# Moving an attention kernel's transposes from TensorE to DMA and its LayerNorm apply from ScalarE to GpSimd

## The chip, the cores and the metric

The kernel runs on one core of a Trainium2 chip. The metric is device time in microseconds (us) of one execution, median over several. Every run quoted here was fast: none was over 1.5% above the fastest run of its kernel.

Words used below: PE is TensorE's matmul, PEld its weight load, DVE is VectorE, ACT is ScalarE, POOL is GpSimd and SP is SyncE. "SPq" and "ACTq" in a profile line are those engines' sequencers issuing a DMA.

## The reference, cut to what matters

Four layers, A B A B, on x of 2048 rows by 576 columns, with x in bf16 and the sums kept in f32:

```python
def _A_ref(x, wqkv, wo):          # attention: 32 heads of 18; a query sees itself and 7 earlier keys, 2 apart
    ...
    idx = pos[:, None] - off[None, :]            # off = 0, 2, ..., 14
    logits = jnp.einsum('bhsd,bhswd->bhsw', q, kg) * scale
    attn = _softmax(jnp.where(mask, logits, -1e9), axis=-1)
    o = jnp.einsum('bhsw,bhswd->bhsd', attn, vg)
    return o.reshape(B, S, D) @ wo

def _B_ref(x, w_in, w_sp, b_sp, w_out):          # mixer
    z = _gelu(x @ w_in)                          # 576 -> 4608
    z1, z2 = z[..., :Fh], _layernorm(z[..., Fh:])
    g = jnp.einsum('ts,bsf->btf', w_sp, z2) + b_sp[None, :, None]
    return (z1 * g) @ w_out

x = x + _A_ref(_layernorm(x), ...)               # then B, then A, then B in the same way
```

## The kernel before

An attention works on tiles of queries against a window of 128 keys. Each tile is done in two steps, one per half of the heads. A step is: scores on PE, Exp on ACT, a multiply with a 0/1 mask on DVE, the product with V on PE, and a normalisation on DVE into `o_t`. The first steps also carry the QKV product and a DMA scatter of Q and K (called "early steps" here). The other 22 steps have Exp split into two halves and "junk" matmuls that keep PE busy ("late steps").

Two transposes happen per tile. The attention output `o_t` is transposed before the output product, and the normalised row `xn` is transposed into `xnT`, the input of the next layer. Before the change both are matmuls against an identity, followed by a DVE copy out of PSUM:

```python
def ln_xn(self, pool, x_t, nrows, rstd, nmr, eng="act"):
    xn = self.bridge.tile([P, 640], bf16, name="ln_xn", tag="ln_xn", bufs=4)
    nc.gpsimd.memset(xn[:nrows, D:640], 0.0)
    if eng == "act":
        nc.scalar.activation(out=xn[:nrows, 0:D], in_=x_t[:nrows, :], func=ACT.Identity,
                             scale=rstd[:nrows, 0:1], bias=nmr[:nrows, 0:1])
    elif eng == "pool":
        nc.gpsimd.tensor_scalar(out=xn[:nrows, 0:D], in0=x_t[:nrows, :], scalar1=rstd[:nrows, 0:1],
                                scalar2=nmr[:nrows, 0:1], op0=ALU.mult, op1=ALU.add)
    ...
def ln_T(self, xn, row0, nrows, evac="dve"):
    tp = self.PT_tile([P, 5, P], bf16, "ln_tp")
    for c in range(5):
        nc.tensor.transpose(tp[:, c, :nrows], xn[:nrows, c * P:(c + 1) * P], self.ident[:nrows, :nrows])
    self.copy_bf16(self.xnT[:, :, PADL + row0:PADL + row0 + nrows], tp[:, :, :nrows], eng=evac)
```

The tail of a tile is spread over the steps after it. TAIL_A transposes `o_t` and loads the residual, TAIL_B makes the output product and the statistics, TAIL_B2 applies the LayerNorm on ACT, and TAIL_C transposes `xn`:

```python
for (off, fn) in ((2, TAIL_A(t)), (3, TAIL_B(t)), (4, TAIL_B2(t)), (6, TAIL_C(t))):
    s_ = plast + off            # steps after the tile's last step
    ...
```

A mixer begins with its input product (lines with `pz`). The first three of its five weight blocks (`win2a`) are loaded long before. The last two (`win2b`) get their space only when the attention's pools close, and one of them is issued on SP and one on ACT:

```python
for c in range(NPF, 5):
    self.dma(win2b[:kc, c - NPF, :], self.B_w_in[...], eng=(nc.sync, nc.scalar)[c % 2])
```

The very first LayerNorm, of the input, is spread over engines too: two row groups of 128 in three are applied on ACT, the third on GpSimd.

The softmax here doesn't subtract the row's maximum and nothing guards it: scores larger than these inputs give would overflow.

## Time and profile before

| | before |
|---|---|
| median of 4 runs | 1367.35 us (1366.06 to 1368.14) |
| profiled execution, span | 1364.2 us |
| PE, DVE, ACT, POOL busy | 92%, 48%, 30%, 20% |

By stage, read from the starts and ends of Exp and of the mixers' matmuls in the timeline (us):

| stage | before |
|---|---|
| start, to the first Exp | 47.6 |
| first attention: early steps / late steps | 66.4 / 72.0 |
| from the end of the last Exp to the end of PE's last wait for `win2b` ("entry") | 17.0 |
| first mixer: input product / spatial product | 78.4 / 330.7 |
| output product and the second attention's QKV | 110.1 |
| second attention: early / late / entry | 63.8 / 71.9 / 15.0 |
| second mixer: input product / rest | 78.4 / 412.9 |

The table of stretches gives for each stretch its length, the busy time and count of PE, PEld, DVE, ACT and POOL, then the clock that was granted to PE, the DMA share and GB/s. These are the start, the late steps and the entry of the first mixer, before:

```profile
0.00:48.00 48.00, 26.67 (x156) 16.84 (x157) 21.69 (x80) 18.57 (x27) 30.50 (x108) 1.00 0.60 183
...
114.00:186.00 72.00, 60.55 (x1052) 47.78 (x1060) 66.08 (x164) 49.78 (x65) 13.17 (x40) 1.00 0.25 66
186.00:203.00 17.00, 8.85 (x66) 6.31 (x67) 9.25 (x24) 3.88 (x4) 2.75 (x8) 0.88 0.41 109
```

In the late steps DVE is busy 66.08 of 72 us and PE 60.55: no engine is quite full. One tile of them in the timeline (columns: start, duration, engine, line and operation, output<-inputs, count, and in brackets how long the engine was idle before it and for whom):

```profile
133.86 1.75 ACT L507 ACTIVATE P_sb_115<-L_ps 128x912 bf16<-128x912 f32 x2 [1.36 <-PE O_ps L540]
...
134.33 0.41 PE L187 MATMUL ln_tp<-ident,ln_xn 114*128 114x114 bf16 x5
...
134.59 0.41 PE L565 MATMUL o_tp<-ident,o_t 114*128 114x114 bf16 x5
...
135.56 0.44 DVE L82 COPY xnT<-ln_tp 128x285 int32<-128x285 int32 x1
...
135.93 0.44 DVE L82 COPY oT_t<-o_tp 128x285 int32<-128x285 int32 x1
...
136.33 0.87 ACT L173 ACTIVATE ln_xn<-x_new,ln_nmr,ln_rstd 114x576 bf16<-114x576 f32 x1 [0.71 <-POOL ln_nmr L164]
...
140.48 0.93 ACT L507 ACTIVATE P_sb_115<-L_ps 128x912 bf16<-128x912 f32 x1 [1.36 <-PE O_ps L540]
```

The same Exp returns after 140.48 − 133.86 = 6.62 us: that is the time of one tile (here and below, the mean over six tiles in the middle of the late steps). Exp waits for PE, PE carries ten transposes, DVE carries two copies of 0.44 us, and ACT itself carries the LayerNorm apply of 0.87 us.

The entry to the first mixer, in the timeline before:

```profile
189.07 2.63 PE L581 MATMUL pw<-wo_sb,oT_t 128*114 128x288 bf16 x10
...
197.75 0.55 SPq L77 DMA_DIRECT2D win2b<-in_B_w_in_dram  x1
197.76 0.35 ACTq L77 DMA_DIRECT2D win2b<-in_B_w_in_dram  x1
...
201.97 0.38 PE L811 MATMUL pz<-win2b,xnT 128*128 128x512 bf16 x1 [3.50 <-DMA win2b<-in_B_w_in_dram]
```

The last weights are issued at 197.75, and PE stands 3.50 us for them, then another 0.67.

Before, the start's GpSimd applies (multiply by `rstd`, add `nmr`) are listed by duration (min/median/max in ns):

```profile
L176 POOL TENSOR_SCALAR ln_xn<-x_in_207,ln_rstd,ln_nmr x2: 820/820/821, 29.7 to 33.3; 128x576 bf16<-128x576 bf16 x2
```

### The profile page before, as it was taken

The numbers are of one execution on the slowest core, as the hardware profiler recorded it, in microseconds if no ns is written. First come the engines' busy times: TensorE is split into PE (matmuls) and PEld (weight loads), VectorE is DVE, ScalarE is ACT, GpSimd is POOL, SyncE is SP. The second block draws the span as 40 slices with busy tenths as digits, with TensorE's granted clock in tenths as the row PEclk, the third lists the DMA queues.
The fourth block names the chain that finished last, engine by engine and source line by source line (L and its number), as shares of the span: only waits on it lengthen the run. The fifth ranks groups of instructions, "written<-read, shape, count | busy, mean of one in ns | idle before, by whom it ended". The sixth has DMA issues, their size and how long they took to land.

```text
span 1364.2 us, 22004 instructions
## 1 busy us (share of the span) xinstructions
PE 1261.8 (92%) x8906; PEld 705.5 (52%) x9008; DVE 653.8 (48%) x1496; ACT 410.5 (30%) x609; POOL 274.5 (20%) x569
## 2 busy tenths in 40 slices
PE   3998869989999999998999888799999999999897
PEld 2566644444444444446865666444444444444476
DVE  5468967853223223333544799688333232332221
ACT  3566647630111111001125666466111111001000
POOL 6422116840000000002241221288100000000011
PEclk9999999999999999997999999999999999999999
DMA  6323239020000000007432332580100000000242
GB/s 211 71 72 85 63 96 230 1 86 9 9 9 10 9 9 9 1 5 247 132 107 69 93 88 80 146 166 18 64 10 9 9 9 5 5 9 0 66 118 65
DMA packets 114469, 85.32 MB, mean 63 GB/s; under 512 B 72616, under 2 KB 96552, under 8 KB 114368
## 3 DMA queue, kind: packets, MB, share of 16 engines
q1 hardware_dynamic: 104548, 68.41, 18.7%
q10 hardware_dynamic: 6364, 8.55, 2.1%
q0 software_dynamic: 3456, 6.96, 2.0%
q8 instruction: 70, 1.15, 0.4%
q14 instruction: 31, 0.25, 0.1%
HBM read 41.16 MB, written 16.52 MB: 42 GB/s over the span
## 4 chain that ended last, share of the span: by engine, by line
PE 66%; DVE 16%; DMA 5%; ACT 5%; POOL 4%; issue 3%; SPq 0%; ACTq 0%; POOLq 0%; DVEq 0%
PE pg L903 35%; PE po L940 9%; PE pp L414 5%; DVE z_junkD L818 4%; DMA QK<-stg 2%; DVE ln_st L157 2%; PE pw L581 1%; POOL z_rstd L834 1%; DMA wout_b<-in_B_w_out_dram 1%; POOL ln_rstd L162 1%; ACT P_sb_116 L507 1%; ACT P_sb_7442 L507 1%; DVE P_sb_7442 L527 1%; DVE x_new L583 1%; PE pv L372 1%
## 5 line engine op out<-in xcount | busy, mean ns | idle before, releaser
L907 DVE TENSOR_TENSOR g_tmp<-pg,bsp 128x512 f32<-128x512 f32 x144 | 99.4, 692 | 434.7 <-PE pg L903 399.1
L811 PEld LDWEIGHTS <-xnT 128*128 128x128 bf16 x800 | 78.1, 98 | 91.9 <-issue 13.7
L414 PE MATMUL pp<-xnT,wqk_sb 128*126 128x512 bf16 (+1 forms) x400 | 100.1, 392 | 6.1 <-ACT xnT L84 4.7
L811 PE MATMUL pz<-win2a,xnT 128*128 128x512 bf16 x380 | 102.6, 379 | 2.0 <-DVE x_new L583 1.6
L811 PE MATMUL pz<-win2b,xnT 128*128 128x512 bf16 x242 | 73.6, 385 | 8.2 <-DMA win2b<-in_B_w_in_dram 7.3
L815 ACT ACTIVATE zp<-pz 128x1024 bf16<-128x1024 f32 x64 | 65.1, 1021 | 51.7 <-POOL z2b_10393 L844 21.9
L414 PEld LDWEIGHTS <-wqk_sb 128*126 128x126 bf16 (+1 forms) x400 | 50.3, 133 | 35.8 <-issue 8.9
L581 PE MATMUL pw<-wo_sb,oT_t 128*114 128x288 bf16 (+1 forms) x360 | 57.4, 297 | 2.1 <-DVE oT_t L82 1.1
L372 PE MATMUL pv<-wv_sb,xnT 128*128 128x288 bf16 x360 | 56.0, 285 | 2.7 <-PE L_ps L492 2.5
L162 POOL TENSOR_TENSOR ln_rstd<-ln_rstd,neg_half 114x1 f32<-114x1 f32 (+1 forms) x68 | 39.2, 578 | 89.1 <-DVE ln_rstd L161 89.0
L818 DVE CUSTOM_DVE_ANT_0 z_junkD<-zp 128x1536 bf16<-128x1536 bf16 x32 | 56.6, 1768 | 1.1 <-ACT zp L815 1.1
L492 PE MATMUL L_ps<-QK 18*128 18x114 bf16 x1152 | 31.9, 212 | 20.0 <-ACT P_sb_7442 L507 5.1
L581 PEld LDWEIGHTS <-oT_t 128*114 128x114 bf16 (+1 forms) x360 | 44.1, 135 | 5.9 <-DVE oT_t L82 1.5
L187 PE MATMUL ln_tp<-ident,ln_xn 114*128 114x114 bf16 (+2 forms) x340 | 29.1, 224 | 17.4 <-ACT ln_xn L173 11.5
L173 ACT ACTIVATE ln_xn<-x_new,ln_nmr,ln_rstd 114x576 bf16<-114x576 f32 (+1 forms) x36 | 31.2, 867 | 46.3 <-POOL ln_nmr L164 46.3
L171 POOL MEMSET ln_xn<- 114x64 bf16 (+1 forms) x68 | 10.8, 161 | 164.2 <-PE ln_tp L187 71.3
L77 POOL DMA_DIRECT2D QK<-stg x52 | 31.5, 606 | 59.8 <-ACT stg L423 43.4
L492 PEld LDWEIGHTS <-QK 18*128 18x128 bf16 x1152 | 21.0, 93 | 43.2 <-issue 38.7
L77 POOL DMA_DIRECT2D wout_b<-in_B_w_out_dram x14 | 7.6, 548 | 172.5 <-PE pg L903 172.5
L372 PEld LDWEIGHTS <-xnT 128*128 128x128 bf16 x360 | 32.6, 97 | 12.6 <-issue 0.4
L82 DVE COPY xnT<-ln_tp 128x285 int32<-128x285 int32 (+2 forms) x60 | 27.3, 458 | 23.6 <-PE ln_tp L187 9.9
L187 PEld LDWEIGHTS <-ln_xn 114*128 114x128 bf16 (+2 forms) x340 | 23.8, 101 | 21.2 <-ACT ln_xn L173 13.4
(504 smaller groups left out, 2558.7 us busy)
## 6 DMA issues: line engine op xcount, KB each, us to landing
xres_74<-x_new SPq DMA_DIRECT2D x17, 256.5 KB
xo<-xres_75 SPq DMA_DIRECT2D x17, 256.5 KB
xres_76<-x_new SPq DMA_DIRECT2D x17, 256.5 KB
QK<-stg POOLq DMA_DIRECT2D x52, 72.0 KB, 3.7
win2a<-in_B_w_in_dram SPq DMA_DIRECT2D x2, 1728.0 KB
QK<-stg SPq DMA_DIRECT2D x48, 72.0 KB
wqk_sb<-in_A_wqkv_dram ACTq DMA_DIRECT2D x4, 576.0 KB
out_dram<-ob SPq DMA_DIRECT2D x16, 144.0 KB
```

Of the source, the lines that this page charges most:

```text
L162: nc.gpsimd.tensor_tensor(out=rstd[:nrows, :], in0=rstd[:nrows, :], in1=self.neg_half[:nrows, :], op=ALU.pow)
L187: nc.tensor.transpose(tp[:, c, :nrows], xn[:nrows, c * P:(c + 1) * P], self.ident[:nrows, :nrows])
L372: nc.tensor.matmul(pv[:, 0:288], lhsT=self.xnT[:, c, QT * t:QT * t + P], rhs=wv_sb[:, c, hh * 288:(hh + 1) * 288], start=(c == 0), stop=(c ...
L414: nc.tensor.matmul(pp[:M, :], lhsT=wqk_sb[:, c, wc0:wc0 + M], rhs=self.xnT[:, c, col0:col0 + 512], start=(c == 0), stop=(c == 4))
L492: nc.tensor.matmul(L_ps[:, j, ftl * QT:(ftl + 1) * QT], lhsT=kT[32 * j:32 * j + DH, g, QT * t:QT * t + P], rhs=qT[32 * j:32 * j + DH, g, Q ...
L581: nc.tensor.matmul(pw[:nq, 0:288], lhsT=oT_t[:, c, :nq], rhs=wo_sb[:, c, hh * 288:(hh + 1) * 288], start=(c == 0), stop=(c == 4))
L811: nc.tensor.matmul(pzvs[ci][:, sub * 512:sub * 512 + w], lhsT=self.xnT[:, c, PADL + i * P:PADL + (i + 1) * P], rhs=win2(c)[:, c0 + sub * 5 ...
L815: nc.scalar.activation(out=zp[:, c0:c0 + cn], in_=pzvs[ci][:, 0:cn], func=ACT.Gelu_apprx_tanh, accum_out=sums[:, ci:ci + 1])
L818: nc.vector.tensor_tensor_reduce(out=junkD[:], in0=zp[:, 0:SQ_D], in1=zp[:, 0:SQ_D], scale=1.0, scalar=0.0, op0=ALU.mult, op1=ALU.add, acc ...
L903: nc.tensor.matmul(pg[:, :], lhsT=z2b[jj][:, i, sub * P:(sub + 1) * P], rhs=W_sb[:, i, q * 512:(q + 1) * 512], start=(i == 0), stop=(i == ...
L907: nc.vector.tensor_tensor(out=tmp[:], in0=pg[:, :], in1=bsp[:, q * 512:(q + 1) * 512], op=ALU.add)
L940: nc.tensor.matmul(acc[hh], lhsT=uT[j // 2][:, j % 2, i * P:(i + 1) * P], rhs=wout_j(j)[:, hh * 288:(hh + 1) * 288], start=(j == 0), stop= ...
```

## The change

The intent is to free PE and DVE of transposes and copies, and ACT of the apply, in the steps where the three are in each other's way. The core of the diff, with cuts:

```diff
-HALO = (W_ATT - 1) * DIL          # 14, so 114 queries per tile
+HALO = 16                         # 112 queries per tile: 19 tiles instead of 18, the last of 32
@@ ln_xn
-        elif eng == "pool":
-            nc.gpsimd.tensor_scalar(out=xn[...], in0=x_t, scalar1=rstd, scalar2=nmr, op0=ALU.mult, op1=ALU.add)
+            e = nc.gpsimd if eng == "pool" else nc.vector
+            e.tensor_scalar(out=xn[...], in0=x_t, scalar1=mv[:nrows, 0:1], scalar2=rstd, op0=ALU.subtract, op1=ALU.mult)
@@ ln_T
-        ... five nc.tensor.transpose and a copy ...
+        self.nc.sync.dma_start_transpose(out=self.xnT[:, :, PADL + row0:PADL + row0 + nrows], in_=xn[:nrows, :])
@@ TAIL_A
-        ... five nc.tensor.transpose and a DVE copy ...
+        nc.sync.dma_start_transpose(out=oT_t[:, :, :nq], in_=o_t[:nq, :])
@@ TAIL_B2
-        st["xn"] = self.ln_xn(sb, x_new, st["nq"], rstd, nmr, eng="act")
+        st["xn"] = self.ln_xn(x_new, st["nq"], mv, rstd, nmr, eng="pool")
@@ steps of the tail
-            ((2, TAIL_A(t)), (3, TAIL_B(t)), (4, TAIL_B2(t)), (6, TAIL_C(t)))
+            ((2, TAIL_A(t)), (4, TAIL_B(t)), (5, TAIL_B2(t)), (6, TAIL_C(t)))
@@ VW (copy of V out of PSUM)
-                if hh == 0:                     # DVE, else ACT
+                if hh == 0 and t % 3 == 0:      # DVE, else ACT
@@ EXP
-                     func=ACT.Exp
+                     func=ACT.Exp, scale=float(scale)     # Q is no longer scaled when it leaves PSUM
@@ weight loads of the QKV and the output product
-                lhsT=wqk_sb[:, c, wc0:wc0 + M]          # 126 or 72 columns
+                lhsT=wqk_sb[:, c, wc0:wc0 + P]          # 128 columns
-                lhsT=oT_t[:, c, :nq]                     # 114 columns
+                lhsT=oT_t[:, c, :]                       # 128 columns
```

The first mixer's output product uses the same `ln_T` and so gets DMA transposes too.

## The prediction

> What bounds the kernel now. The table of stretches splits the 1364 us into first attention 0-197, first mixer to 700, second attention to 866, second mixer. The mixer's spatial and output products (PE 97-99% busy) are over half the time and keep their work. The change lives in the two attentions (~365 us) and at the seams.
>
> In the second half of each attention the timeline repeats every 6.62 us per tile (two steps). Matmuls pitch at 0.122 us (288 wide) and 0.216 us (512 wide), so PE really issues about 5.3 us of that: output product and V product 1.2 each, junk 0.86, ten transposes 0.54, the rest scores and PV. DVE is busy 93% (32.5 of 35 us). The list of waits shows Exp (1.75 us) then standing 1.36 us for PV behind junk and output product, and every other Exp behind the LayerNorm apply on ScalarE (0.87 us), itself behind GpSimd. So it is a chain through in-order PE, DVE and ScalarE, not one full engine.
>
> Per tile the change removes ten transposes (0.54 us PE), two DVE copies (0.44 us each), the 0.87 us apply on ScalarE, and moves two in three of one 0.45 us V copy from DVE to ScalarE (0.40). It adds about 0.9 us on GpSimd (the apply took 0.82 there on bf16) and two DMA transposes. The 16 weight transposes of 512 KB took 38 us, so I estimate 0.7 us of DMA time per 160 KB plus about 2 us fixed latency (the Trainium skill, "DMA: Bandwidth & Descriptors", Anatomy of one DMA); the tail has one more step of slack for it. The program order puts scores right after each Exp, ahead of output product and junk. I expect 5.3-5.6 us per tile: 10 full tiles save ~12 us per attention, less 3 us for the extra 32-query tile (19 instead of 18). The first 14 (now 16) steps are limited by QKV matmuls and scatter; I expect the same length there.
>
> 128-wide weights: loads of 126 and 114 columns take 133-135 ns against 98, but the steady pitch of both groups equals that of full-width ones, so under 2 us in all.
>
> Elsewhere: each output-product row group of the first mixer pays 0.28 us for five transposes: 4.5 us, plus 1.5 us at its end (PE waits 1.15 us for a copy). Entering each mixer, the last input weights are issued only after the last residual store lands and PE waits some 5 us; in the new order they wait for matmuls and queue slots only: 4 us saved each, reduced by the DMA latency of the last tiles. At the start, transposes queue behind a 1.7 MB weight load (x issued just after it landed 9 us later): first QKV matmul 3-5 us later, repaid by 80 transposes gone from PE. Net zero.
>
> Sum: 2x10 + 6 + 8 + ~5 (early-phase PE and PSUM slots) = about 39-42 us. Predicted 1326 us, 80% range 1302 to 1354; faster by over 2% 0.72, within 2% 0.21, slower 0.07.
>
> Right if: late Exp starts 5.3-5.7 us apart per tile; DVE copies and transposes gone; mixer time unchanged; PE idle entering mixers shorter; pitches unchanged.
>
> Wrong if: PE waits for DMA at the output product (transposes from SBUF slower than from HBM, or the in-order SP queue holding them behind stores and scatters); the scatter of Q and K lands later because of them and delays early steps; GpSimd's apply holding the port against the two-input mask multiply (the Trainium skill, "SBUF — State Buffer", Who interferes with whom; here GpSimd's first mixer apply took 1.93 us against 0.65-0.7 for the others); or the start slips by 10 us.

## The result, and the profile after

| | before | after |
|---|---|---|
| median of 4 runs | 1367.35 us (1366.06 to 1368.14) | 1348.38 us (1347.21 to 1350.22) |
| ratio, 95% interval | | 0.986 (0.9846 to 0.9874) |

A ratio here is the mean time of one kernel's fast runs over the mean of the other's fast runs of the same rounds, so it is not quite the ratio of the medians. The change makes the kernel 1.4% faster: 19 us where 41 were predicted. The predicted range of 1302 to 1354 us holds the 1348, but the class called likeliest (faster by over 2%) was wrong.

The stages of the two profiled executions (us). The early steps are 14 before and 16 after, because a tile is smaller; the late ones are 22 in both, but after the last two belong to the tile of 32 queries. The executions differ by 15.8 us, because the profiled run of before was its fastest (1366.06) and that of after its slowest (1350.22):

| stage | before | after | difference |
|---|---|---|---|
| start | 47.6 | 51.7 | +4.1 |
| early steps, both attentions | 130.2 | 124.0 | −6.2 |
| late steps, both | 143.9 | 123.9 | −20.0 |
| entries, both | 32.0 | 39.7 | +7.7 |
| input products, both | 156.8 | 159.6 | +2.8 |
| output product and QKV | 110.1 | 105.8 | −4.3 |
| spatial product and the rest | 743.6 | 743.8 | +0.2 |

The same three stretches after:

```profile
0.00:52.00 52.00, 23.50 (x111) 10.12 (x112) 20.01 (x75) 16.21 (x24) 36.20 (x96) 0.97 0.81 212
...
115.00:175.00 60.00, 54.65 (x922) 36.92 (x921) 53.43 (x131) 40.83 (x60) 35.60 (x24) 1.00 0.73 122
175.00:195.00 20.00, 10.32 (x80) 6.05 (x77) 9.56 (x30) 0.13 (x1) 11.91 (x9) 0.83 0.50 129
```

The late steps lost 12 us with DVE at 53.43 of 60 us, so the aimed-at gain is there. But POOL in that stretch went from 13.17 to 35.60 us, and in the entry from 2.75 to 11.91 us. The part of the page that follows back the chain which ended last says the same. Before:

```profile
PE 66%; DVE 16%; DMA 5%; ACT 5%; POOL 4%; issue 3%; SPq 0%; ACTq 0%; POOLq 0%; DVEq 0%
```

After:

```profile
PE 62%; DVE 11%; POOL 10%; issue 7%; DMA 6%; ACT 3%; SPq 1%; ACTq 0%; POOLq 0%; DVEq 0%
PE pg L904 36%; PE po L941 9%; DVE z_junkD L819 4%; PE pp L412 3%; DMA QK<-stg 2%; POOL ln_xn_84 L181 2%; POOL ln_xn_81 L181 1%; POOL ln_rstd L164 1%; POOL z_rstd L835 1%; POOL ln_xn_83 L181 1%; POOL ln_xn_82 L181 1%; DMA wout_b<-in_B_w_out_dram 1%; DMA wv_sb<-in_A_wqkv_dram 1%; DMA win2b<-in_B_w_in_dram 1%; DVE z_msq L828 1%
```

GpSimd's share of that chain rose from 4% to 10%, and the LayerNorm apply (`ln_xn`, line 181) is named four times in it. Its durations after:

```profile
L181 POOL TENSOR_SCALAR ln_xn_81<-x_new,ln_mv,ln_rstd x10: 2290/2296/3209, 90.7 to 847.8; 112x576 bf16<-112x576 f32 x10
...
L181 POOL TENSOR_SCALAR ln_xn_82<-x_in_100,ln_mv,ln_rstd x1: 2289/2289/2289, 22.5 to 22.5; 128x576 bf16<-128x576 bf16 x1
```

The second line is the telling one: the same engine, shape and types as the 820 ns apply of before now take 2289 ns. What differs is the pair of operations with its scalars: subtract the mean and multiply by `rstd`, in place of multiply by `rstd` and add `nmr`. (The 3209 ns of the first line is a second effect, which the first experiment explains.)

A late tile in the timeline after (the one apply follows the other after 148.58 − 142.77 = 5.81 us; the mean over six tiles is 5.83):

```profile
142.77 2.29 POOL L181 TENSOR_SCALAR ln_xn_82<-x_new,ln_mv,ln_rstd 112x576 bf16<-112x576 f32 x1
...
144.22 1.20 SPq L568 DMA_TRANSPOSE oT_142<-o_t_130  x1
...
145.50 1.23 SPq L186 DMA_TRANSPOSE xnT<-ln_xn_82  x1
...
148.58 2.29 POOL L181 TENSOR_SCALAR ln_xn_83<-x_new,ln_mv,ln_rstd 112x576 bf16<-112x576 f32 x1
```

The ten transposes and the two DVE copies are gone. In this steady state the slow apply does no visible harm, since there is one per 5.8 us and its result is wanted only a step later. SP needs 1.2 us to issue one transpose, where the plain copies around it take 0.4 to 0.6 us.

The entry to the first mixer is where it does harm. The timeline after:

```profile
176.55 2.29 POOL L181 TENSOR_SCALAR ln_xn_84<-x_new,ln_mv,ln_rstd 112x576 bf16<-112x576 f32 x1
...
178.87 1.19 SPq L186 DMA_TRANSPOSE xnT<-ln_xn_84  x1
...
180.16 1.21 SPq L568 DMA_TRANSPOSE oT_142<-o_t_129  x1
...
182.70 2.58 PE L582 MATMUL pw<-wo_sb,oT_142 128*128 128x288 bf16 x10 [3.96 <-DMA oT_142<-o_t_129]
...
187.46 2.29 POOL L181 TENSOR_SCALAR ln_xn_82<-x_new,ln_mv,ln_rstd 112x576 bf16<-112x576 f32 x1
...
189.78 1.19 SPq L186 DMA_TRANSPOSE xnT<-ln_xn_82  x1
...
191.09 0.55 SPq L76 DMA_DIRECT2D win2b<-in_B_w_in_dram  x1
...
195.01 1.25 PE L812 MATMUL pz<-win2b,xnT 128*128 128x512 bf16 x5 [3.64 <-DMA win2b<-in_B_w_in_dram]
```

Read it upwards from PE's two waits. PE stands 3.96 us for the transposed attention output `oT_142`. Its source `o_t_129` was complete at about 176.4 us, but SP issues in program order, and the transpose of `ln_xn_84` comes first there. That one waits for the GpSimd apply, which ends at 178.84. (Spans on GpSimd are rough, but SP's issue at 178.87 confirms this end.) SP then spends 1.2 us on it, so `oT_142` is issued at 180.16 and PE starts at 182.70. The second wait has the same shape: `win2b` stands on SP behind the transpose of `ln_xn_82`, which waits for the apply that ends at 189.75. ACT's half of `win2b` had been issued at 187.11; SP's half follows at 191.09.

The clock comes on top, but the kernel before paid most of this too. After the 3.96 us gap the ten matmuls take 2.58 us, against 1.39 us for the same ten of the tile before (at 174.78 us). Before, the product in the same place took 2.63 us. The Trainium skill, "TensorE: Matmul & The Clock Gate", section "HAM oscillation — how this bites in real kernels", gives the rule of no PE-idle gaps over about 3.4 us. These traces don't bear it out as a threshold. After, the granted clock halves at about 179.5 us, only 0.7 us into the gap, behind a stretch in which PE had little work. Before, it halves at about 188.6 us, 2.7 us into a gap of 2.80 us, behind a PE that had been busy. It stays halved for 6.8 us after (to about 186.3) and for 3.4 us before (to about 192.0, and once more from 202.2 us).

The start after, up to the second group of QKV matmuls:

```profile
21.32 1.26 SPq L186 DMA_TRANSPOSE xnT<-ln_xn_84  x1
...
25.21 4.32 PE L412 MATMUL pp<-xnT,wqk_sb 128*128 128x512 bf16 x10 [25.21 <-DMA xnT<-ln_xn_84]
...
28.02 1.38 SPq L186 DMA_TRANSPOSE xnT<-ln_xn_84  x1
...
32.81 1.44 PE L412 MATMUL pp<-xnT,wqk_sb 128*128 128x512 bf16 x3 [3.29 <-DMA xnT<-ln_xn_84]
```

Before, these two starts were at 23.14 and 30.18 us. A transpose is used 3.9 and 4.8 us after SP began to issue it (25.21 − 21.32, 32.81 − 28.02), against 2.5 us in the tail above (182.70 − 180.16). The prediction's estimate of about 0.7 plus 2 us fits the tail and is too short for the start. (The section that it names gives its 2 us for DMAs issued by GpSimd; these are issued by SP.)

### The profile page after: what moved, and what is told of

It reads as the page before. It is cut to its first block, busy times and chain, and to the rows that moved or that the text cites. A ratio compares the mean times of both kernels' runs of the same rounds, so it can differ in the third digit from the quotient of the medians.

```text
span 1348.4 us, 21451 instructions
## 1 busy us (share of the span) xinstructions
PE 1249.9 (93%) x8656; PEld 659.5 (49%) x8656; DVE 616.5 (46%) x1402; ACT 384.2 (28%) x595; POOL 356.4 (26%) x487
## 4 chain that ended last, share of the span: by engine, by line
PE 62%; DVE 11%; POOL 10%; issue 7%; DMA 6%; ACT 3%; SPq 1%; ACTq 0%; POOLq 0%; DVEq 0%
PE pg L904 36%; PE po L941 9%; DVE z_junkD L819 4%; PE pp L412 3%; DMA QK<-stg 2%; POOL ln_xn_84 L181 2%; POOL ln_xn_81 L181 1%; POOL ln_rstd L164 1%; POOL z_rstd L835 1%; POOL ln_xn_83 L181 1%; POOL ln_xn_82 L181 1%; DMA wout_b<-in_B_w_out_dram 1%; DMA wv_sb<-in_A_wqkv_dram 1%; DMA win2b<-in_B_w_in_dram 1%; DVE z_msq L828 1%
## 5 line engine op out<-in xcount | busy, mean ns | idle before, releaser
L412 PE MATMUL pp<-xnT,wqk_sb 128*128 128x512 bf16 x400 | 100.7, 394 | 29.8 <-DMA xnT<-ln_xn_84 28.5
L812 PEld LDWEIGHTS <-xnT 128*128 128x128 bf16 x800 | 78.4, 98 | 97.0 <-issue 13.0
L164 POOL TENSOR_TENSOR ln_rstd<-ln_rstd,neg_half 112x1 f32<-112x1 f32 (+2 forms) x70 | 43.4, 621 | 152.3 <-DVE ln_rstd L163 152.1
L412 PEld LDWEIGHTS <-wqk_sb 128*128 128x128 bf16 x400 | 36.9, 100 | 71.2 <-issue 36.0
L370 PE MATMUL pv<-wv_sb,xnT 128*128 128x288 bf16 (+1 forms) x380 | 62.2, 286 | 0.2 <-DVE stg L418 0.2
L584 DVE TENSOR_TENSOR x_new<-pw,xo 112x288 f32<-112x288 f32 (+1 forms) x76 | 33.5, 445 | 18.0 <-PE pw L582 10.7
L370 PEld LDWEIGHTS <-xnT 128*128 128x128 bf16 (+1 forms) x380 | 33.5, 97 | 15.8 <-issue 1.4
L489 PE MATMUL L_ps<-QK 18*128 18x112 bf16 (+1 forms) x1216 | 32.0, 210 | 4.9 <-DMA QK<-stg 1.7
L159 DVE BATCH_NORM_STATS2 ln_st<-x_new 112x6 f32<-112x288 f32 (+1 forms) x76 | 33.9, 449 | 1.2
L845 POOL TENSOR_SCALAR z2b_3101<-zp,z_rstd,z_nmr 128x256 bf16<-128x256 bf16 x16 | 32.4, 2024 | 0.0
L845 POOL TENSOR_SCALAR z2b_9746<-zp,z_rstd,z_nmr 128x256 bf16<-128x256 bf16 x16 | 32.4, 2023 | 0.0
```

The lines of the kernel that those rows point to most:

```text
L164: nc.gpsimd.tensor_tensor(out=rstd[:nrows, :], in0=rstd[:nrows, :], in1=self.neg_half[:nrows, :], op=ALU.pow)
L370: nc.tensor.matmul(pv[:nk, 0:288], lhsT=self.xnT[:, c, QT * t:QT * t + nk], rhs=wv_sb[:, c, hh * 288:(hh + 1) * 288], start=(c == 0), stop ...
L412: nc.tensor.matmul(pp[:, :], lhsT=wqk_sb[:, c, wc0:wc0 + P], rhs=self.xnT[:, c, col0:col0 + 512], start=(c == 0), stop=(c == 4))
L489: nc.tensor.matmul(L_ps[:nk, j, ftl * QT:ftl * QT + nq], lhsT=kT[32 * j:32 * j + DH, g, QT * t:QT * t + nk], rhs=qT[32 * j:32 * j + DH, g, ...
L812: nc.tensor.matmul(pzvs[ci][:, sub * 512:sub * 512 + w], lhsT=self.xnT[:, c, PADL + i * P:PADL + (i + 1) * P], rhs=win2(c)[:, c0 + sub * 5 ...
L845: nc.gpsimd.tensor_scalar(out=z2b[b][:, i, :], in0=zp[:, b * 256:(b + 1) * 256], scalar1=rstd[:, 0:1], scalar2=nmr[:, 0:1], op0=ALU.mult, ...
```

## The experiments

My theory: (1) the tile time fell as predicted in kind; (2) the gain is given back at the seams, because GpSimd's apply takes 2.29 us instead of 0.8, and everything that SP issues in order behind it (transposes, last weights) inherits the delay; (3) the cause of the 2.29 us is the pair of operations. Rivals: the apply is slow because it shares a memory port with DVE's mask multiply, or because its input is f32; the DMA transposes themselves are too slow for the seams whatever GpSimd does; or the gain was the wider weight loads' and not the transposes'. All twelve runs gave correct results. The time before, in the three groups of runs, was 1364.37, 1367.22 and 1368.62 us (medians of 7 runs each).

### Multiply and add on GpSimd

```diff
-   e.tensor_scalar(..., scalar1=mv[:nrows, 0:1],   scalar2=rstd[:nrows, 0:1], op0=ALU.subtract, op1=ALU.mult)
+   e.tensor_scalar(..., scalar1=rstd[:nrows, 0:1], scalar2=nmr[:nrows, 0:1],  op0=ALU.mult,     op1=ALU.add)
```

(and `nmr`, one small GpSimd operation, is computed for every row group again)

> The changed kernel with only the GpSimd apply written as multiply-then-add (scale and bias prepared by one small GpSimd operation, as the kernel before had it) instead of subtract-then-multiply. Program order on TensorE is the same. If the form of the operation is what made the apply 2.29 us where the same 128x576 took 0.82 before, it falls to 0.8-0.95 us; if it is slowed by VectorE holding a shared port, it stays near 2.3. First theory (the apply stands on the chain into each mixer, behind it the in-order transpose queue): each entry (last Exp to the first matmul with the late weights) falls from 19.9 to about 17 us, the tile period from 5.8 to 5.6-5.7, the whole from 1348 to about 1340. Rival (GpSimd is off the critical path): within 2 us of 1348.

Measured: 1336.04 us, ratio to before 0.9799 (0.9779 to 0.9819). Durations of the apply in this run:

```profile
L181 POOL TENSOR_SCALAR ln_xn<-x_new,ln_rstd,ln_nmr x38: 805/816/2035, 91.9 to 837.2; 112x576 bf16<-112x576 f32 x36, 32x576 bf16<-32x576 f32 x2
L181 POOL TENSOR_SCALAR ln_xn<-x_in,ln_rstd,ln_nmr x5: 806/815/817, 11.1 to 50.4; 128x576 bf16<-128x576 bf16 x5
```

The median is 816 ns with the f32 input and 815 ns with bf16, so the type did not make it slow. Nor did the port: at the start, where no mask multiply has run yet, the apply takes 815 ns here and 2289 ns in the change. The operation pair with its scalars did. But the port has an effect of its own, which the median hides. During 13 of the 36 applies of 112 rows a whole mask multiply runs, and these 13 take 1.94 to 2.04 us:

```profile
123.88 1.94 POOL L181 TENSOR_SCALAR ln_xn<-x_new,ln_rstd,ln_nmr 112x576 bf16<-112x576 f32 x1
124.05 1.08 DVE L527 TENSOR_TENSOR P_sb<-P_sb,mask_base 128x1792 bf16<-128x1792 bf16 x1
```

The other 23 take 0.81 to 0.82 us: the apply grows by about the 1.08 us of the mask multiply. In the change too, the 9 applies beside which a mask multiply began at nearly the same time (within 0.15 us) grew to 3.1 to 3.2 us, one of them (172.20 to 175.41 us) just ahead of the first entry. Where the mask multiply began 0.5 us or more later, the apply kept its 2.29 us.

The entries fell from 19.9 and 19.8 us to 15.9 and 16.2 us, and the tile time from 5.83 to 5.73 us. This one edit is worth another 0.6%. The start stayed at 51.4 us.

### The last weights on ScalarE's queue

```diff
-   self.dma(win2b[...], ..., eng=(nc.sync, nc.scalar)[c % 2])
+   self.dma(win2b[...], ..., eng=nc.scalar)
```

> The changed kernel with the second part of the late mixer input weights issued on ScalarE's queue like the first part, not behind the transposes on SP's. If its place in SP's order is what ends the entry, it is issued near 187 us instead of 191.1 and each entry falls by about 4 us, the whole by 7-8 us to about 1340. If something else ends the entry (the output product of the last tiles waiting for its transposes), it falls by less than 2 us each.

Measured: 1343.06 us, 0.9845 (0.9829 to 0.9862). The entries are 16.4 and 16.6 us, 3.5 and 3.2 us shorter, but the interval overlaps that of the change (0.9846 to 0.9874), so the 7 to 8 us expected of the whole are a miss. The timeline of PE shows why little of it arrives. After the weights come earlier, the input product soon waits for something else:

```profile
191.55 0.59 PE L812 MATMUL pz<-win2b,xnT 128*128 128x512 bf16 x2 [0.39 <-DMA win2b<-in_B_w_in_dram]
...
196.30 0.81 PE L812 MATMUL pz<-win2a,xnT 128*128 128x512 bf16 x3 [1.56 <-ACT zp L816]
```

The 3.64 us for `win2b` became 0.39, and the 0.36 us wait for ACT's Gelu (`zp`) became 1.56. The input product grew by 1.3 and 0.9 us (80.7 and 81.1). The rest of the difference stays within what two profiles scatter.

### TensorE transposes for the last two tiles' attention output

```diff
+   if t >= NT - 2:
+       ... five nc.tensor.transpose of o_t and a DVE copy, as before ...
+   else:
        nc.sync.dma_start_transpose(out=oT_t[:, :, :nq], in_=o_t[:nq, :])
```

> The changed kernel with the attention output of only the last two tiles of each attention transposed on TensorE. First theory: the 3.96 us that TensorE waits for the transposes of these tiles, which stand in SP's order behind a transpose that waits for GpSimd, are gone, and each entry falls by 3 to 4 us, the whole by 6-8 us to about 1341. Rival (the entry is bound by the LayerNorm chain and the weights' issue after it): the wait moves on to the weights and each entry falls by under 1.5 us.

Measured: 1333.59 us, 0.9779 (0.9759 to 0.9799). The entries are 13.7 and 15.6 us. The apply is still the slow one here. PE's timeline shows the transposes in gaps that PE had anyway, and the output product no longer waits for a DMA:

```profile
177.02 0.26 PE L571 MATMUL o_tp<-ident,o_t 112*128 112x112 bf16 x2
...
179.75 1.03 PE L588 MATMUL pw<-wo_sb,oT 128*128 128x288 bf16 x7
```

The output product starts at 179.75 instead of 182.70 us. Leaving SP's queue at the seam is worth about as much as curing the apply. In the profiled pair the entries account for some 10 us; this run's rest of the second mixer was also 3.7 us shorter, which I do not claim for the edit.

### Every transpose on TensorE, the slow apply kept

All `dma_start_transpose` of `o_t` and `xn` are undone, everything else of the change stays, the new order of the tail too.

> The changed kernel with every transpose of activations back on TensorE, all else of the change kept (112-query tiles, GpSimd apply, full-width loads, scale in Exp). Prices the DMA transposes. If they are what the gain comes from: tile period 5.8 to about 6.4 us, each row group of the first mixer's output product 0.28 us longer, entries 3-4 us shorter, the start a few us earlier; the whole about 1360-1366, as slow as before. If the gain comes from the rest of the change (the apply moved off ScalarE), it stays under 1352.

Measured: 1418.15 us, 1.0394 (1.0375 to 1.0413). I had expected about 1360 to 1366: a miss by over 50 us. The group of LayerNorm transposes shows the cause (busy us and mean ns, then idle time of PE just before them and what ended it):

```profile
L190 PE MATMUL ln_tp<-ident,ln_xn 112*128 112x112 bf16 (+2 forms) x350 | 33.0, 231 | 70.9 <-POOL ln_xn L181 52.2
```

PE stands 52.2 us for the apply. PE runs in order, and a transpose on PE that waits for GpSimd holds up all matmuls behind it. With DMA transposes it is SP that waits, and PE goes on. The tile time here is 9.12 and 8.23 us. So the apply on GpSimd was hidden in the change only because of the DMA transposes. (TensorE transposes with the fast multiply-and-add apply on GpSimd were not run.)

### Every transpose on TensorE, the apply back on ScalarE

As the last, and `eng="act"` in TAIL_B2, with multiply and add in the start's GpSimd applies.

> The run with all transposes on TensorE came out at 1418 us, far over the 1360-1366 expected. Theory: there TensorE, in order, waits for the 2.3 us GpSimd apply at every LayerNorm transpose (52 us of waits in its profile), so DMA transposes are what makes the slow apply tolerable. This run keeps all transposes on TensorE but takes the apply of the attention tail back to ScalarE as before (and multiply-then-add for the few GpSimd ones of the first LayerNorm). It then has of the change only 112-query tiles, full-width loads, scale in Exp and the V copies. Expected 1364-1376 us, ratio to the kernel before 1.00-1.01, tile period about 6.6. Rival (the 112-query tiling or the layout itself costs): stays above 1395.

Measured: 1375.54 us, 1.0065 (1.0036 to 1.0094). The total is as expected, but the tile time of 7.47 us is not: it should have been near 6.6. What is left of the change in this kernel therefore costs 0.85 us per tile, which the next one takes apart.

### The same with the old order of the tail and the old V copies

```diff
-   ((2, TAIL_A(t)), (4, TAIL_B(t)), (5, TAIL_B2(t)), (6, TAIL_C(t)))
+   ((2, TAIL_A(t)), (3, TAIL_B(t)), (4, TAIL_B2(t)), (6, TAIL_C(t)))
-   if hh == 0 and t % 3 == 0:
+   if hh == 0:
```

> The version with every transpose on TensorE and every LayerNorm apply of the tail on ScalarE, which took 7.47 us per late tile against 6.62 before, now also with the tail's steps (3, 4 after the tile instead of 4, 5) and the V copies (all of the first half on VectorE) as before. If the new step order and the V copies on ScalarE cost the 0.85 us: 6.6 to 6.8 us per late tile and a ratio to the kernel before of 0.99 to 1.00. If the 112-query tile itself or the other buffers cost it: 7.3 us or more and 1.005 or more.

Measured: 1361.27 us, 0.9943 (0.9918 to 0.9968), with a tile time of 6.63 us (6.62 before). So the 112-query tile, the folded scale, the fixed buffers and the wide loads together leave the tile time alone. The new order of the tail, with two in three of the first-half V copies on ACT, costs 1.2% of the time before (1.0065 against 0.9943) while the transposes are on PE and the apply is on ACT. I did not part the two. The change's order is made for DMA transposes, and with both a tile takes 5.83 us; the old order with DMA transposes was not run, so it is not shown that the new one pays there.

This run shows two more things. From the first to the end of the last Exp its attentions take 3.2 and 1.0 us longer than before, which is what the extra tile costs here. And its entries are 12.3 and 13.4 us, against 17.0 and 15.0 before: with the transposes on PE, 4.7 and 1.6 us of the 4 us that the prediction counted at each entry do appear (the last weights go out at 195.69 us, ahead of the last residual store at 196.39).

### The old widths of the weight loads

```diff
-   nc.tensor.matmul(pp[:, :], lhsT=wqk_sb[:, c, wc0:wc0 + P], ...)
+   nc.tensor.matmul(pp[:M, :], lhsT=wqk_sb[:, c, wc0:wc0 + M], ...)
-   nc.tensor.matmul(pw[:, 0:288], lhsT=oT_t[:, c, :], ...)
+   nc.tensor.matmul(pw[:nq, 0:288], lhsT=oT_t[:, c, :nq], ...)
```

> The changed kernel with only the weight loads put back to their old widths (126 or 72 columns for the QKV product, 112 for the output product). My theory: the loads hide under the stream, so the time is that of the changed kernel, 1346 to 1351 us, ratio to the kernel before 0.984 to 0.989, while the mean of one such load goes up from about 98-100 to about 133 ns. Rival: the wide loads are worth a good part of what was gained, then 1355 us or more.

Measured: 1349.88 us, 0.9858 (0.9823 to 0.9893), the same as the change (0.986). The groups of loads in this run (busy us, mean ns):

```profile
L413 PEld LDWEIGHTS <-wqk_sb 128*126 128x126 bf16 (+1 forms) x400 | 51.7, 138 | 60.2 <-issue 34.9 <-DVE ln_st L159 0.2
L583 PEld LDWEIGHTS <-oT 128*112 128x112 bf16 (+1 forms) x380 | 46.5, 135 | 17.6 <-DMA oT<-o_t 10.6 <-issue 2.5
```

After the change the first group reads:

```profile
L412 PEld LDWEIGHTS <-wqk_sb 128*128 128x128 bf16 x400 | 36.9, 100 | 71.2 <-issue 36.0 <-DVE ln_mv L161 0.3
```

The wide loads are faster, 100 ns against 138, and none of it reaches the time. The Trainium skill, "TensorE: Matmul & The Clock Gate", section "Weight-path perf modes — Fast Weight Load (FWL) and DoubleRow", says that the fast load is on when the number of weights is 128 and the type is not FP32. The durations agree in direction (138 to 100 ns, less than the page's measured gain of about two times). But the loads are hidden under the matmuls, at a pitch of 0.216 us for 512 columns before.

### TensorE transposes for the first eight row groups

```diff
-   self.ln_T(xns.pop(i), i * P, P)
+   self.ln_T(xns.pop(i), i * P, P, pe=(("dve" if i % 2 == 0 else "act") if i < 8 else None))
```

> The changed kernel with the first 8 row groups of the first LayerNorm transposed on TensorE, the other 8 by DMA. Theory: the start loses 4.1 us (first Exp at 51.7 against 47.6) because the transposes stand in SP's queue, 1.2 us of issue each, behind 3.5 MB of loads, and TensorE waits for the 4th and 8th. Expected: first Exp near 46-48 us, whole 4-5 us shorter than the changed kernel, ratio about 0.983. Rival (the start is lost to GpSimd's slow apply of every third row group): first Exp stays within 1.5 us of 51.7.

Measured: 1346.85 us, 0.9863 (0.9827 to 0.9899), and the first Exp at 51.7 us, unmoved: a miss. PE's timeline of this run:

```profile
20.14 1.51 PE L190 MATMUL ln_tp<-ident,ln_xn 128*128 128x128 bf16 x10 [6.44 <-DVE ln_rstd L163]
25.15 4.42 PE L419 MATMUL pp<-xnT,wqk_sb 128*128 128x512 bf16 x10 [3.50 <-ACT xnT L83]
...
32.70 12.64 PE L419 MATMUL pp<-xnT,wqk_sb 128*128 128x512 bf16 x50 [2.02 <-ACT xnT L83]
```

The QKV matmuls start at 25.15 and 32.70 us, as with DMA transposes. Two causes gave the same time, each enough by itself, so taking one away showed nothing. The next run takes both.

### The same with multiply and add

> The changed kernel with TensorE transposes for the first eight row groups AND the GpSimd LayerNorm apply as multiply/add. It asks why TensorE transposes alone did not shorten the start. If it was the slow GpSimd apply that the in-order TensorE waited for: first Exp at 47 to 49 us (51.7 changed, 51.4 with multiply/add alone, 51.7 with TensorE transposes alone), time 1330 to 1334 us, 3 us under multiply/add alone. If the gain in the best version so far came from its end-of-attention edits instead: first Exp stays at 51 us or more and the time stays at about 1336.

Measured: 1334.12 us, 0.9752 (0.9728 to 0.9776); the first Exp is at 48.8 us. PE's timeline:

```profile
18.75 1.51 PE L190 MATMUL ln_tp<-ident,ln_xn 128*128 128x128 bf16 x10 [5.43 <-DVE ln_rstd L163]
22.64 4.42 PE L419 MATMUL pp<-xnT,wqk_sb 128*128 128x512 bf16 x10 [2.38 <-ACT xnT L83]
...
29.72 4.48 PE L419 MATMUL pp<-xnT,wqk_sb 128*128 128x512 bf16 x20 [1.22 <-ACT xnT L83]
```

The two starts are at 22.64 and 29.72 us. The slow apply alone, or the DMA transposes alone (51.4 us in the first experiment), each keep the start at 51 to 52 us; without both it is 48.8.

### The seam edits together, and a version that beats both kernels

Together: multiply and add; TensorE transposes of the last two tiles' output; ScalarE for the last three tiles' apply (`eng=("act" if t >= NT - 3 else "pool")`); the last weights on ScalarE's queue.

> The changed kernel with the entry mended at all places: attention output of the last two tiles transposed on TensorE, LayerNorm apply of the last three tiles on ScalarE (idle there), the late weights on ScalarE's queue, GpSimd's apply as multiply-then-add. If the three waits stand one behind the other, the gains add: entries from 19.9 to 10-12 us, tile period 5.73, ratio 0.969-0.973. If they overlap (one chain, whichever is longest), entries no shorter than 13 us and ratio 0.975-0.978.

Measured: 1327.24 us, 0.9712 (0.9682 to 0.9742). The first Exp is at 52.7 us, the entries are 13.1 and 14.4 us, and the input products 79.3 and 79.3 us. The first product on `win2b` comes at 11.0 and 12.2 us, but PE then waits once more for the other half of the weights; the 19.9 us of the change were counted to the end of that last wait. By the same count the entries came out as the rival said (no shorter than 13 us), though the ratio lies in the theory's range. The three edits shortened the entries by 13.7 and 11.0 us in sum when each was alone, and by 6.8 and 5.4 us here: the waits overlap. The profiled run's second mixer behind its input product, which no experiment edits, was 4.3 us shorter than that of the change, so the total cannot decide this.

With the TensorE transposes of the first eight row groups as well:

> The version to beat both kernels: the mended entry and the first 8 row groups transposed on TensorE. Expected the sum of the two: ratio 0.965-0.970, about 1318-1324 us.

Measured: 1324.17 us, 0.9677 (0.9647 to 0.9707). The first Exp is at 48.4 us, the entries are 13.6 and 13.1 us, and the input products 79.5 and 79.8 us (79.4 and 80.2 after).

And without the weights' edit:

> The best version so far (1324 us: TensorE transposes in the first eight row groups and for the last two tiles, multiply/add apply, ScalarE apply for the last three tiles, last mixer weights all on the ScalarE queue) without its last edit: the last mixer weights go back to alternate between the two queues. If the weights' edit is worth something here: entries 2 to 4 us longer each, 1327 to 1331 us. If it only moved time from the entry into the product behind it (79 to 82 us there): that product back to 79-80 us and a time within 2 us of 1324.

Measured: 1322.40 us, 0.9660 (0.9634 to 0.9685). The entries are 13.4 and 13.4 us and the input products 79.6 and 80.3 us, as with the edit. PE's last wait for `win2b` in the first mixer, with the edit and without it:

```profile
183.46 1.47 PE L825 MATMUL pz<-win2b,xnT 128*128 128x512 bf16 x6 [0.98 <-DMA win2b<-in_B_w_in_dram]
...
183.60 1.68 PE L825 MATMUL pz<-win2b,xnT 128*128 128x512 bf16 x7 [1.65 <-DMA win2b<-in_B_w_in_dram]
```

It ends at the same time in both, so the weights' edit does nothing here: SP's half is issued at 178.61 us without it, no longer held behind a late transpose, and the second half goes out at 179.16 us with it. (The expectation's "time moved into the product" came of counting the entry to the first product on `win2b` in one version and to the last wait in the other.) The two versions' intervals overlap, so the edit is left out as useless, not as harmful. This is the best version measured: about 2% under the change and 3.4% under the kernel before.

## Why the prediction was wrong, point by point

- **Late steps, "2x10" us saved.** Right in the sum, 11.8 and 8.2 us, but by luck: the tile time of 5.83 us lies above the predicted 5.3 to 5.6, so the ten full tiles saved 8.4 and 4.8 us and not 12 each. The rest, 3.4 us each, is that the last tile of the stage now has 32 queries; the prediction had counted that tile as 3 us lost.
- **Early steps, "~5" us.** Near: 6.2, with 16 steps instead of 14. The prediction's text had "the same length there"; only its sum counted the 5 us.
- **Output product of the first mixer, 6 us.** Nearly right: 4.3.
- **Wide loads, under 2 us.** Right: no difference could be measured.
- **"4 us saved each, reduced by the DMA latency of the last tiles" at the mixers' entries.** This is the step that failed. The sum took the full 8; the entries became 2.9 and 4.8 us longer. That is 15.7 us of the missing gain. The prediction saw that the last weights would no longer wait for a residual store. It did not follow SP's order to the end: in the last tiles each DMA transpose stands behind another whose source is still with GpSimd, and the weights stand behind them all. The multiply/add run (−4.0 and −3.6 us) and the TensorE transposes of the last two tiles (−6.2 and −4.2 us) each cut the entries by themselves; together, with the ScalarE apply for the last tiles besides, they come to 13.4 and 13.4 us, below before. So most of the 4 us were there to be had, but not in this form; the run with everything on PE in the old order had 4.7 and 1.6 us of them.
- **"About 0.9 us on GpSimd".** The mis-sized term beneath that step: it measured 2.29 us. I took the 0.82 us of the same engine, shape and types, and did not look at the pair of operations, which the diff shows to be another. In the late steps this cost only some 0.1 us per tile (5.83 against 5.73); at the entries it cost about half of what was lost (the multiply-and-add run took 7.6 of the 15.7 us back).
- **The start, "net zero".** It lost 4.1 us. Transposes behind loads and the slow apply are each enough to cause it, as the pair of start experiments showed.
- **Input products, "mixer time unchanged".** They grew by 1.0 and 1.8 us; that cause is not settled.
- **What was feared.** "PE waits for DMA at the output product" came true, but only in the last tiles. The port that GpSimd shares with VectorE was the other fear. The Trainium skill, "SBUF — State Buffer", section "Who interferes with whom", calls the port pair of VectorE and GpSimd an exclusive lock. The traces agree in part. A mask multiply that begins together with the apply holds it for about its own length (0.81 becomes 1.94 us, 2.29 becomes 3.2). But one that begins 0.5 us into the 2.29 us apply is itself held for little, 1.25 us instead of 1.08, and not until the apply ends. So what the prediction feared for VectorE fell mostly on GpSimd. Its own 1.93 us was a sign of this: of the mixer's three applies on GpSimd the last takes 1.93 us in the mean, beside a two-input operation of VectorE (`z_junkD`), and the others 0.6 to 0.7. Late scatters did not delay the early steps, which became shorter.

The sum: 20.0 + 6.2 + 4.3 gained, 4.1 + 7.7 + 2.8 + 0.2 lost, 15.7 us in the profiled pair (15.8 by the spans).

What stays open: how much of the 1.2% (new tail order and V copies, with the transposes on PE) belongs to the V copies; whether the new order pays with DMA transposes; and why the input products grow in some variants beyond the Gelu wait that was shown.

## What to carry to other kernels

A move off a busy engine pays in the steady state and is paid for at the seams, so cost a change there separately: follow each in-order queue, that of the DMA issuer too, to the first instruction whose source is late. A duration may be borrowed from the trace only for the same operation, and the two arithmetic operations of an instruction are part of that, as is what VectorE does beside it. Where two causes can each hold a start by themselves, undo them together before calling either innocent.

## What the Trainium skill lacked or had wrong

- "GPSIMD Engine Reference", section "4.1 Engine selection", calls one-input elementwise work on GpSimd roughly line-rate, and no page gives the cost by pair of operations. The runs show 2.29 us for subtract and multiply with per-partition scalars, and 0.81 us for multiply and add, on the same 128x576 bf16 tile and in the same place of the kernel. No run here shows why.
- "DMA: Bandwidth & Descriptors", section "Issuing engines are not separate DMA queues", calls the time of initiating a DMA usually small relative to the DMA itself. For the SBUF-to-SBUF transposes of 112 rows by 640 columns here the issue took 1.2 us on SP, against 0.4 to 0.6 us for plain copies beside them, and the result was used 2.5 us after the issue began: half of it is issue. No page gives a measured issue time of such a small transpose on this chip.
- The same page places a semaphore wait on the issuing sequencer, but gives no example of what that costs the DMAs behind it when a transpose waits for its source: here the last weights' issue moved from 187.11 us (the half on ScalarE's queue) to 191.09 us (the half on SP's).
- "TensorE: Matmul & The Clock Gate", section "HAM oscillation — how this bites in real kernels", gives about 3.4 us as the limit of a gap. Here the clock halved 2.7 us into a gap of 2.80 us (before), and 0.7 us into one of 3.96 us behind sparse work (after).
